# A recurrent attention block and an MLP in one kernel: twelve of sixteen sign steps of the weight conversion move from ScalarE to VectorE, more idle matmuls at the start, and a new written order for all engines

## The chip, the cores and the metric

One core of a Trainium2 chip. The time is device microseconds of one execution. The kernel before has a median of 570.65 us over 6 runs (570.09 to 571.48). The profile is of one execution of 571.31 us.

## The reference

```python
# gated linear attention, B=4, H=8, S=768, D=48, float32
state = zeros(B, H, D, D)
for t in range(S):
    state = alpha[:, :, t, :, None] * state + einsum('bhd,bhe->bhde', k[:, :, t], v[:, :, t])
    y[:, :, t] = einsum('bhd,bhde->bhe', q[:, :, t], state)
x = y.transpose(0, 2, 1, 3).reshape(3072, 384)
# MLP
h = x @ w_in                      # w_in 384 x 2048, float64 as handed in
g = h * clip(h + 3, 0, 6) / 6
out = g @ w_out                   # w_out 2048 x 384, float64 as handed in
```

The two weight matrices come as 64-bit floats. [...]the kernel loads each number as two 32-bit words and makes the float32 itself.

## The kernel before

**Chunks and groups.** The sequence is cut into 24 chunks j of 128 tokens (6 per batch); two chunks are a group g of 256 tokens, 12 groups. A chunk goes through the attention, a group through the MLP. All is float32.

**Attention of a chunk.** The scan of the decays is done within a chunk by VectorE: `r` (line 301, a scan backward, and a reciprocal in line 305) and `p` (line 312, a scan forward), then `k` and `q` scale the transposed keys and queries (line 324). TensorE makes the scores `sc` (line 332); VectorE masks them, `m` (line 338); TensorE makes the output within the chunk, `yi` (line 426), and from the carried state, `yx` (line 436); `kb` and `u` with VectorE's `sm` and GpSimd's `st` (line 383) carry the state. ScalarE copies the result to SBUF, `cy`. The first 6 chunks are transposed by TensorE (`ta`, `tk`, `tq`, line 274), later ones by VectorE (line 278).

**Weights.** They come in 16 slices of 128 x 768 numbers, 768 KB each: 0 to 7 are w_in (`w.0` to `w.7`, four DMAs each, line 174), 8 to 15 are w_out (one DMA each, line 177). A slice lands in one of five places, 0, 1, 2, 3, 4, 0, 1, 2 for slices 0 to 7 (3 and 4 lie in a tile, g_sb, that is free at the start), and 0, 1, 2 in turn after that; so slice 5 waits until slice 0 has been converted, 6 for 1, 7 for 2, 8 for 5, and so on. The conversion of slice i, with the names of the written order:

- `d2` (line 200, ScalarE): the size of the high word, read as a float, times 2^16, into the weight's place
- `d1` (line 189, ScalarE): the low word, scaled and rounded to an integer, in place
- `dx` (line 195, ScalarE): the sign of the high word, kept as a 16-bit half beside the low word
- `d3` (lines 208 and 209, VectorE): the size is clamped and shifted left by 3 bits
- `d4` (line 214, GpSimd): an integer add of low word and high part gives the float32

**MLP of groups 0 and 1.** These run while the weights arrive, as plain products. Step `f.g.i` (line 457) multiplies group g with slice i of w_in: 12 matmul records of 256 columns; `fa` and `fb` (line 468) do it for one chunk of group 0 at a time. ScalarE's `fr` and VectorE's `fg` apply the gate. Steps `b` (line 495) are w_out for group 0.

**MLP of the later groups.** It uses fewer products of sums. As the last `f` and `b` steps go by, VectorE turns w_in and w_out into sums in place: `y` (25 steps, lines 516 to 520) and `x.0` to `x.3` (line 626). From group 2 on the first matrix is the steps `M` (line 579, 128 columns), with sums of the inputs `xc` and of the results `o`; from group 1 on the second is the steps `P` (line 679, 192 columns), with sums `s`, copies `K`, outputs `G` and stores `O`.

**What sets the order.** One string of words near the end of the file (`run`), one word per step, gives the order in which the instructions of every engine and every DMA queue are issued; each engine works through its own in that order, and waits at the first whose inputs are not ready. All loads are issued by SP, one after the other; the stores by ScalarE's queue. The word `z.m.n` is `idle`: n matmuls whose result nobody reads, into PSUM bank m.

Of the kernel before, what the change touches and what calls it, by code (L numbers as in the profile page):

```python
# [17 lines left out]
def kernel(  # L18
# [32 lines left out]
    nc = tc.nc  # L51
# [81 lines left out]
    LOWEST, HIGHEST = 2.0, 2.0**16 * (122880.0 - 2.0**-7)  # L133
# [46 lines left out]

    def slice_of(i):
        dst, raw = weight_dst(i), raw_of(i)
        lo, hi = (raw[:, :, x].rearrange("p (m n) -> p m n", m=dst.shape[1]) for x in range(2))
        return dst, lo, hi
# [6 lines left out]
    def sign(i):  # L191

        dst, _, hi = slice_of(i)
        halves = raw_of(i).bitcast(F16).rearrange("p (m n) h -> p m n h", m=dst.shape[1])
        nc.scalar.activation(out=halves[:, :, :, 1], in_=hi.bitcast(I32), func=AF.Copy,
                             scale=2.0**-64)

    def magnitude(i):
        dst, _, hi = slice_of(i)
        nc.scalar.activation(out=dst, in_=hi.bitcast(FP), func=AF.Abs, scale=2.0**16)  # L200

    def magnitude_bits(i):

        dst, _, _ = slice_of(i)
        bits = dst.bitcast(U32)
        nc.vector.tensor_scalar(dst, dst, LOWEST, HIGHEST, ALU.max, ALU.min)
        nc.vector.tensor_single_scalar(bits, bits, 3, op=ALU.logical_shift_left)

    def add_low(i):

        dst, lo, _ = slice_of(i)
        nc.gpsimd.tensor_tensor(out=dst.bitcast(I32), in0=dst.bitcast(I32), in1=lo.bitcast(I32),  # L214
                                op=ALU.add)
# [291 lines left out]
    def idle(m, n):  # L507

        for _ in range(n):
            nc.tensor.matmul(bank_m[m][:, 0:C], ones[:, 0:C], ones[:, 0:C], start=True,  # L510
                             stop=True)
# [185 lines left out]
    def store2(g, i):  # L697
# [9 lines left out]
        "d1": round_low, "d2": magnitude, "dx": sign, "d3": magnitude_bits, "d4": add_low,  # L707
# [11 lines left out]
    def run(words):  # L719
        for word in words.split():  # L720
            name, *at = word.split(".")
            steps[name](*(int(x) for x in at))

    with tc.manual_schedule():
        run("""la.0 lk.0 lq.0 lk.1 ta.0 la.1 tk.0 la.2 ca.0 r.0 tq.0 lv.3.0 tk.1 lq.1 k.0 p.0 ta.1
            la.3 ca.1 ta.2 lv.0.1 q.0 ca.2 r.1 sc.0 lq.3 tq.1 lk.2 k.1 p.1 ta.3 la.4 z.0.2 r.2
            lv.1.2 ca.3 kb.0 w.1 z.0.1 q.1 ck.0 m.0 tk.2 u.0 k.2 sc.1 sm.0 p.2 tq.3 kb.1 lq.2
            z.0.2 m.1 st.1 ck.1 lk.3 ta.4 r.3 u.1 w.0 ca.4 yi.0 d2.1 sm.1 d1.1 d3.1 tq.2 z.0.1
            cy.0 dx.1 tk.3 q.2 st.2 lv.2.1 sc.2 k.3 d4.1 lq.5 kb.2 m.2 fa.1.0 w.2 r.4 d2.0 yi.1
            d1.0 d3.0 yx.1 dx.0 z.1.2 p.3 cy.1 w.3 fb.1 d4.0 q.3 sc.3 fr.0.1 p.4 d2.2 fa.0.1  # L730
            fg.0.1 d1.2 w.4 d3.2 tq.5 ck.2 fb.0 dx.2 m.3 d4.2 u.2 fr.0.0 yi.3 sm.2 d2.3 fg.0.0
            fa.2.2 st.3 lk.5 d1.3 d3.3 w.5 dx.3 yx.3 fb.2 cy.3 d4.3 d2.4 yi.2 d1.4 d3.4 tk.5
            fr.0.2 yx.2 lv.4.2 dx.4 fg.0.2 f.0.3.3 w.6 cy.2 d4.4 d2.5 f.1.2.0 d1.5 d3.5 fr.0.3
            la.5 dx.5 fg.0.3 w.7 f.1.3.1 d4.5 fr.1.2 fg.1.2 d2.6 d1.6 f.0.5.2 d3.6 fr.1.3 w.8
            dx.6 fg.1.3 d4.6 fa.4.3 fr.0.5 fg.0.5 kb.3 d2.7 fb.4 d1.7 d3.7 w.9 dx.7 f.0.6.0
            fr.0.4 d4.7 fg.0.4 d2.8 f.1.7.1 d1.8 d3.8 lk.4 fr.0.6 w.10 dx.8 fg.0.6 ck.3 f.1.6.2
            d4.8 fr.1.7 d2.9 fg.1.7 d1.9 d3.9 f.1.1.3 w.11 dx.9 fr.1.6 d4.9 fg.1.6 tk.4 d2.10
            ta.5 k.4 f.1.0.0 d1.10 w.12 d3.10 ca.5 dx.10 r.5 fr.1.1 u.3 fr.1.0 fg.1.1 d4.10
            f.0.7.1 d2.11 sm.3 lv.5.1 d1.11 k.5 st.4 fg.1.0 lq.4 dx.11 d3.11 f.1.5.2 fr.0.7 w.13
            fg.0.7 d4.11 d2.12 d1.12 b.0.0.3 d3.12 fr.1.5 dx.12 fg.1.5 w.14 d4.12 tq.4 f.1.4.0  # L740
            q.4 p.5 d2.13 d1.13 q.5 w.15 sc.4 d3.13 fr.1.4 dx.13 sc.5 m.4 d4.13 b.0.1 d2.14 m.5
            d1.14 la.6 d3.14 dx.14 kb.4 b.0.2 fg.1.4 d4.14 ck.4 lq.6 d2.15 d1.15 d3.15 u.4
            lv.6.0 dx.15 yi.5 sm.4 d4.15 lk.6 b.1.0.1 ca.6 r.6 lq.7 b.0.3 x.0 p.6 la.7 b.1.1
            tk.6 st.5 bo.0 so.0 y.1 k.6 y.5 yi.4 kt.6 b.1.2 y.6 kw.6 y.2 y.3 y.7 yx.4 y.4 y.8
            b.1.3 cy.4 tq.6 y.9 y.10 yx.5 y.11 bo.1 kr.6 x.1 P.1.1.2 so.1 cy.5 lk.7 s.1.0.0 x.2
            P.1.0.0 lv.7.1 s.1.1.1 la.8 x.3 M.2.15.3 K.1.0 s.1.2.2 u.6 P.1.3.1 s.1.3.3 s.1.4
            y.13 y.15 P.1.2 K.1.2 y.16 y.0 y.17 xc.2.1 y.12 M.2.16 K.1.1 xc.2.3 y.19 P.1.4
            xc.2.4 G.1.0 xc.2.5 O.1.0 y.20 s.1.5 M.2.0.2 q.6 G.1.1 sc.6 y.18 O.1.1 xc.2.6 y.21
            P.1.6 tq.7 y.23 xc.2.0 ca.7 P.1.5 G.1.3 xc.2.7 O.1.3 r.7 xc.2.8 p.7 M.2.7.0 n.2.0.8
            xc.2.9 M.2.1 sm.6 n.2.7.9 tk.7 st.7 M.2.8 n.2.1.10 o.2.4.0 M.2.2 k.7 e.2.4 M.2.17  # L750
            xc.2.2 xc.2.10 n.2.2.11 kt.7 M.2.3 y.14 kw.7 q.7 M.2.4 y.22 sc.7 G.1.2 n.2.4.12 y.24
            O.1.2 o.2.0.0 M.2.18.1 m.6 e.2.0 lq.8 M.2.9 n.2.18.13 h.2.0 M.2.5 o.2.1.0 M.2.19
            h.2.4 n.2.5.14 e.2.1 m.7 kr.7 M.2.10 M.2.6.2 lv.8.2 h.2.1 n.2.10.15 ca.8 yi.6 lk.8
            o.2.6.0 M.2.11 cy.6 r.8 yi.7 n.2.11.12 lq.9 o.2.5.0 M.2.12 p.8 e.2.5 yx.7 n.2.12.9
            h.2.5 u.7 la.9 cy.7 M.2.13 o.2.3.0 o.2.7.0 P.2.0.1 n.2.13.11 o.2.3.1 o.2.2.0 e.2.3
            o.2.7.1 h.2.3 e.2.7 M.2.14 o.2.2.1 K.2.0 h.2.7 e.2.2 M.3.15.3 o.2.6.1 h.2.2 e.2.6
            M.3.16 s.2.1.15 P.2.1.2 h.2.6 s.2.3.9 s.2.0.13 tq.8 P.2.3.0 s.2.2.11 s.2.4 tk.8
            P.2.2 K.2.2 xc.3.1 k.8 xc.3.3 kt.8 xc.3.4 kw.8 G.2.0 xc.3.5 O.2.0 s.2.5 M.3.0.2
            K.2.1 P.2.4 q.8 n.3.0.14 xc.3.6 tq.9 xc.3.0 ca.9 M.3.1 G.2.1 r.9 O.2.1 P.2.6
            n.3.1.12 kr.8 xc.3.7 p.9 lk.9 xc.3.8 M.3.2 sm.7 G.2.3 O.2.3 xc.3.9 sc.8 xc.3.2  # L760
            xc.3.10 n.3.2.10 q.9 lv.9.0 st.8 M.3.7.1 m.8 la.10 u.8 n.3.7.8 M.3.3 sm.8 M.3.8
            o.3.4.0 st.9 tk.9 e.3.4 M.3.4 h.3.4 P.2.5 n.3.4.13 k.9 o.3.0.0 kt.9 e.3.0 h.3.0
            M.3.9 kw.9 G.2.2 ca.10 sc.9 O.2.2 o.3.1.0 M.3.18.0 r.10 e.3.1 M.3.10 n.3.18.15 lq.10
            h.3.1 M.3.5 n.3.10.9 m.9 M.3.19 n.3.5.11 p.10 M.3.11 kr.9 M.3.6.2 o.3.6.0 n.3.11.8
            o.3.5.0 lv.10.1 M.3.17 o.3.7.0 e.3.5 lk.10 M.3.12 o.3.7.1 h.3.5 yi.8 e.3.7 n.3.12.13
            h.3.7 yi.9 lq.11 o.3.3.0 M.3.13 s.3.1.10 o.3.3.1 yx.9 n.3.13.15 s.3.3.9 la.11 yx.8
            e.3.3 o.3.2.0 cy.9 M.3.14 h.3.3 cy.8 o.3.2.1 u.9 o.3.6.1 P.3.0.0 e.3.2 tq.10 e.3.6
            h.3.2 h.3.6 P.3.1.3 tk.10 K.3.0 s.3.0.8 k.10 s.3.2.13 M.4.15.2 s.3.4 P.3.2 kt.10
            xc.4.1 kw.10 G.3.0 xc.4.3 O.3.0 s.3.5 P.3.3.1 K.3.1 xc.4.4 q.10 xc.4.5 tq.11 xc.4.6
            M.4.0.3 xc.4.0 K.3.2 ca.11 P.3.4 n.4.0.15 xc.4.7 r.11 kr.10 xc.4.8 p.11 lk.11 M.4.1  # L770
            G.3.1 sc.10 xc.4.9 O.3.1 sm.9 n.4.1.11 xc.4.2 P.3.6 xc.4.10 lv.11.2 q.11 m.10 st.10
            la.12 M.4.2 G.3.3 tk.11 O.3.3 lq.12 u.10 n.4.2.12 M.4.7.0 k.11 sm.10 M.4.3 n.4.7.14
            st.11 lv.12.0 M.4.16 ca.12 lk.12 M.4.4 o.4.4.0 M.4.8 r.12 n.4.4.9 e.4.4 sc.11 lq.13
            o.4.0.0 P.3.5 h.4.4 e.4.0 m.11 la.13 h.4.0 p.12 M.4.9 M.4.5 G.3.2 o.4.1.0 O.3.2
            M.4.18.1 tk.12 e.4.1 n.4.5.13 M.4.10 h.4.1 n.4.18.8 k.12 M.4.6.3 n.4.10.10 o.4.6.0
            M.4.19 kt.12 M.4.11 ca.13 kw.12 M.4.17 o.4.5.0 n.4.11.14 r.13 yi.10 e.4.5 M.4.12
            h.4.5 o.4.7.0 yi.11 n.4.12.9 o.4.7.1 M.4.13 o.4.3.0 e.4.7 yx.11 o.4.3.1 n.4.13.12
            h.4.7 yx.10 kr.12 e.4.3 o.4.2.0 cy.11 M.4.14 lk.13 h.4.3 cy.10 P.4.0.1 o.4.2.1
            s.4.1.10 e.4.2 o.4.6.1 lv.13.1 h.4.2 e.4.6 s.4.3.8 M.5.15.2 la.14 K.4.0 h.4.6
            P.4.1.3 tq.12 s.4.0.9 xc.5.1 s.4.2.14 s.4.4 u.12 P.4.2 xc.5.3 G.4.0 xc.5.4 O.4.0  # L780
            s.4.5 xc.5.5 P.4.3.0 q.12 K.4.1 xc.5.6 p.13 tq.13 M.5.0.3 K.4.2 xc.5.0 xc.5.8 xc.5.7
            P.4.4 xc.5.9 sm.12 n.5.0.12 tk.13 st.13 ca.14 M.5.1 k.13 G.4.1 sc.12 xc.5.2 O.4.1
# [107 lines left out]
```

## Time and profile before

| what | us |
|---|---|
| median of the runs | 570.65 |
| the profiled execution | 571.31 |
| its span, from the first to the last instruction | 569.5 |
| TensorE busy with matmuls | 550.2 |
| VectorE busy | 469.4 |
| ScalarE busy | 216.7 |
| GpSimd busy | 55.4 |

The granted TensorE clock has a mean of 0.997 over the span. Times in the tables are from the span's start. In a row of the costliest groups stand the line, the engine, the operation, what it writes and reads, the count, then the busy time in us and the mean of one in ns, then the idle time of that engine just before these instructions and what ended most of it. In the order of time, a row is start, duration, engine, line, and in brackets the idle time before it and what ended that. A busy TensorE row is not TensorE at its peak, since matmuls overlap. Each matmul of float32 leaves two records.

### The profile page before, as it was taken

What the parts mean: (1) busy time and instruction counts of PE and PEld (TensorE: products, weight loads), DVE (VectorE), ACT (ScalarE), POOL (GpSimd) and SP (SyncE); (2) the same over time, 40 slices, a digit from 0 to 9 for tenths busy, and PEclk for the clock granted to TensorE, in tenths of its full rate; (3) what the DMA queues carried; (4) which work ended last, traced back from release to release, by engine and by line L of the source; (5) the groups of instructions that cost most, each with busy time, mean ns of one, the idle gap of its engine ahead of it and who ended that gap; (6) DMA issues with size and microseconds to landing.
All of it is one profiled execution on the core that took longest, in us unless ns stands there. A gap on an engine that the chain in (4) does not pass through costs nothing.

```text
span 569.5 us, 12659 instructions
## 1 busy us (share of the span) xinstructions
PE 550.2 (97%) x5196; PEld 506.0 (89%) x5196; DVE 469.4 (82%) x786; ACT 216.7 (38%) x360; POOL 55.4 (10%) x70
## 2 busy tenths in 40 slices
PE   5699899999999999999999999999999999999997
PEld 3587786589999999989989989899899999999997
DVE  7785478999999999899699799989799787564580
ACT  2469999111442432341341341432431431442420
POOL 2225344300000000000001001000000000000000
PEclk9989999999999999999999999999999999999999
DMA  9999777440524535551650655041642630000000
GB/s 146 190 202 179 199 197 184 96 103 21 111 51 97 119 72 115 129 102 33 151 102 16 141 111 141 12 114 23 139 102 61 128 93 8 2 22 8 1 28 22
DMA packets 121270, 53.73 MB, mean 94 GB/s; under 512 B 80636, under 2 KB 114172, under 8 KB 121212
## 3 DMA queue, kind: packets, MB, share of 16 engines
q1 hardware_dynamic: 114588, 48.19, 41.7%
q10 hardware_dynamic: 6624, 4.72, 2.6%
q8 instruction: 41, 0.67, 0.5%
q14 instruction: 17, 0.14, 0.1%
HBM read 44.24 MB, written 8.65 MB: 93 GB/s over the span
## 4 chain that ended last, share of the span: by engine, by line
PE 72%; DVE 10%; DMA 9%; SPq 3%; issue 2%; ACT 2%; DVEq 0%; ACTq 0%
PE m_ps L679 30%; PE m_ps L579 28%; DMA raw<-in_moe_w_in_dram 4%; PE sc_ps L332 3%; PE y_ps L426 3%; PE m_ps L457 3%; PE y_ps L436 2%; DMA rings<-in_k_dram 1%; DMA g_sb<-in_moe_w_in_dram 1%; PE u_ps L396 1%; SPq L174 1%; SPq L253 1%; PE m_ps L495 1%; DMA kq<-in_k_dram 1%; DMA rings<-in_alpha_dram 1%
## 5 line engine op out<-in xcount | busy, mean ns | idle before, releaser
L679 PE MATMUL m_ps<-w,g_sb 128*128 128x192 f32 x704 | 121.7, 328 | 0.4 <-DVE g_sb L516 0.4
L679 PEld LDWEIGHTS m_ps<-w,g_sb 128*128 128x128 f32 x704 | 113.8, 190 | 2.2 <-issue 1.0
L585 ACT COPY g_sb<-m_ps 128x512 f32<-128x512 f32 x110 | 63.7, 583 | 108.5 <-PE m_ps L579 101.8
L679 PE MATMUL m_ps<-rings,g_sb 128*128 128x192 f32 x528 | 92.0, 327 | 0.0
L679 PEld LDWEIGHTS m_ps<-rings,g_sb 128*128 128x128 f32 x528 | 85.4, 190 | 0.7
L473 ACT ACTIVATE r<-g_sb,half 128x512 f32<-128x512 f32 x80 | 57.3, 722 | 75.0 <-DVE g_sb L520 28.0
L579 PE MATMUL m_ps<-xc,w 128*128 128x128 f32 x640 | 84.3, 278 | 0.5 <-DVE oh L695 0.5
L579 PEld LDWEIGHTS m_ps<-xc,w 128*128 128x128 f32 x640 | 78.1, 192 | 3.5 <-issue 1.4
L477 DVE SCALAR_TENSOR_TENSOR g_sb<-r,g_sb 128x512 f32<-128x512 f32 x80 | 54.5, 684 | 17.2 <-ACT r L473 13.0
L383 POOL TENSOR_TENSOR t<-t,R 128x384 f32<-128x384 f32 x20 | 19.6, 978 | 384.6 <-DVE t L411 261.9
L579 PE MATMUL m_ps<-xT,raw 128*128 128x128 f32 x400 | 51.7, 276 | 0.1
L579 PEld LDWEIGHTS m_ps<-xT,raw 128*128 128x128 f32 x400 | 48.7, 192 | 0.5 <-ACT g_sb L585 0.3
L579 PE MATMUL m_ps<-xT,w 128*128 128x128 f32 x320 | 42.1, 279 | 0.1
L626 DVE TENSOR_TENSOR g_sb<-g_sb 128x512 f32<-128x512 f32 (+1 forms) x55 | 41.5, 788 | 0.1
L579 PEld LDWEIGHTS m_ps<-xT,w 128*128 128x128 f32 x320 | 38.2, 192 | 2.0 <-ACT g_sb L585 1.3
L457 PE MATMUL m_ps<-xT,w 128*128 128x256 f32 x144 | 32.4, 381 | 1.6 <-POOL w L214 1.6
L338 DVE TENSOR_TENSOR A<-sc_ps,mask 128x512 f32<-128x512 f32 x48 | 30.7, 682 | 3.9 <-PE sc_ps L332 3.7
L579 PE MATMUL m_ps<-xc,raw 128*128 128x128 f32 x240 | 32.4, 278 | 0.2 <-DVE xc L518 0.2
L312 DVE TENSOR_TENSOR_SCAN P<-t 128x516 f32<-128x516 f32 x24 | 32.4, 1350 | 0.3
L516 DVE TENSOR_TENSOR g_sb<-g_sb 128x512 f32<-128x512 f32 x40 | 27.2, 682 | 6.5 <-ACT g_sb L585 6.5
L301 DVE TENSOR_TENSOR_SCAN R<-t,ones 128x516 f32<-128x516 f32 x24 | 30.4, 1265 | 2.0 <-ACT t L292 1.9
L457 PEld LDWEIGHTS m_ps<-xT,w 128*128 128x128 f32 x144 | 26.9, 190 | 5.7 <-POOL w L214 2.0
(104 smaller groups left out, 704.8 us busy)
## 6 DMA issues: line engine op xcount, KB each, us to landing
raw<-in_moe_w_out_dram SPq DMA_DIRECT2D x8, 768.0 KB, 4.3
t<-in_v_dram SPq DMA_DIRECT2D x48, 96.0 KB, 5.7
raw<-in_moe_w_in_dram SPq DMA_DIRECT2D x24, 192.0 KB, 8.0
out_dram<-oh ACTq DMA_DIRECT2D x44, 96.0 KB, 2.1
far<-kq SPq DMA_DIRECT2D x60, 64.0 KB, 2.3
kb<-far SPq DMA_DIRECT2D x15, 256.0 KB
aq<-in_alpha_dram SPq DMA_DIRECT2D x36, 96.0 KB, 4.0
qq<-in_q_dram SPq DMA_DIRECT2D x36, 96.0 KB, 2.8
```

Of the source, the lines that this page charges most:

```text
L301: nc.vector.tensor_tensor_scan(out=reverse(R, n - 1, n), data0=reverse(ax, n, n), data1=reverse(ones, n, n), initial=0.0, op0=ALU.mult, op ...
L312: nc.vector.tensor_tensor_scan(out=P_t[j], data0=aX[j % 2][:, 0:n], data1=ini[j % 2], initial=0.0, op0=ALU.mult, op1=ALU.add)
L338: nc.vector.tensor_tensor(out=A_t[j][:, NP * o : NP * (o + 1)], in0=ps_t.pop(("sc%d" % o, j)), in1=mask.unsqueeze(1).to_broadcast([C, NP, ...
L383: nc.gpsimd.tensor_tensor(out=st[j % 2], in0=sm[j % 2], in1=R_t[j][:, :, 0:1].to_broadcast([C, NP, 2 * D]), op=ALU.mult)
L457: nc.tensor.matmul(h[:, f], w1[:, kk, o : o + C], xT_t[g][:, kk], start=(kk == 0), stop=(kk == KT - 1))
L473: nc.scalar.activation(out=to, in_=h, func=AF.Relu, bias=half, scale=1.0 / 6.0)
L477: nc.vector.scalar_tensor_tensor(out=to, in0=r, scalar=1.0, in1=h, op0=ALU.min, op1=ALU.mult)
L516: eng.tensor_tensor(out=out, in0=in0, in1=in1, op=ALU.add if s1 > 0 else ALU.subtract)
L579: nc.tensor.matmul(acc[g][i][:, f * C : (f + 1) * C], spots[w][:, f * C : (f + 1) * C], x_of(g, x), start=(first and f == 0), stop=last, s ...
L585: nc.scalar.copy(out=slots[z], in_=acc[g][i])
L626: nc.vector.tensor_tensor(out=out, in0=in0, in1=in1, op=ALU.subtract)
L679: nc.tensor.matmul(to[g], a, rhs[:, f], start=(first and f == 0), stop=(last and f == HF - 1), skip_group_check=True)
```

## The change

Three edits.

1. For slices 0, 1, 2 and 4 the conversion stays as it was. For the other twelve `dx` is left out: `d2` takes the size without the factor, `d3` clamps it, shifts it and masks two bits in the same instruction, and a third VectorE instruction (scalar_tensor_tensor, 128 x 768 words of 32 bits) puts sign and top bit of the high word over it, written to the high word's place, every second word. `d4` then reads the high part from there.
2. The matmuls of `idle` multiply the identity matrix instead of a part of `ones` that is zero; there are 8 such steps with 28 matmuls instead of 5 with 8, the first of them right after the first load is issued.
3. The string with the order of the steps is another one. Its steps are the same, but for the twelve `dx` and the idle ones.

```diff
+    BY_HALVES = {0, 1, 2, 4}
+
...
     def magnitude(i):
         dst, _, hi = slice_of(i)
-        nc.scalar.activation(out=dst, in_=hi.bitcast(FP), func=AF.Abs, scale=2.0**16)
-
-    def magnitude_bits(i):
...
-        dst, _, _ = slice_of(i)
+        nc.scalar.activation(out=dst, in_=hi.bitcast(FP), func=AF.Abs,
+                             scale=2.0**16 if i in BY_HALVES else 1.0)
+
+    def high_bits(i):
+        dst, _, hi = slice_of(i)
         bits = dst.bitcast(U32)
-        nc.vector.tensor_scalar(dst, dst, LOWEST, HIGHEST, ALU.max, ALU.min)
-        nc.vector.tensor_single_scalar(bits, bits, 3, op=ALU.logical_shift_left)
+        if i in BY_HALVES:
+            nc.vector.tensor_scalar(dst, dst, 2.0**16 * LOWEST, 2.0**16 * HIGHEST, ALU.max,
+                                    ALU.min)
+            nc.vector.tensor_single_scalar(bits, bits, 3, op=ALU.logical_shift_left)
+        else:
+            nc.vector.tensor_scalar(dst, dst, LOWEST, HIGHEST, ALU.max, ALU.min)
+            nc.vector.tensor_scalar(bits, bits, 3, 0x3FFFFFF8, ALU.logical_shift_left,
+                                    ALU.bitwise_and)
+            nc.vector.scalar_tensor_tensor(hi, hi, 0xC0000000, bits, ALU.bitwise_and,
+                                           ALU.bitwise_or)
 
     def add_low(i):
 
-        dst, lo, _ = slice_of(i)
-        nc.gpsimd.tensor_tensor(out=dst.bitcast(I32), in0=dst.bitcast(I32), in1=lo.bitcast(I32),
-                                op=ALU.add)
+        dst, lo, hi = slice_of(i)
+        high = dst if i in BY_HALVES else hi
+        nc.gpsimd.tensor_tensor(out=dst.bitcast(I32), in0=high.bitcast(I32),
+                                in1=lo.bitcast(I32), op=ALU.add)
...
         for _ in range(n):
-            nc.tensor.matmul(bank_m[m][:, 0:C], ones[:, 0:C], ones[:, 0:C], start=True,
-                             stop=True)
+            nc.tensor.matmul(bank_m[m][:, 0:C], ident, ident, start=True, stop=True)
```

The constants LOWEST and HIGHEST lose their factor of 2^16. Of the order, the loads up to the last slice of w_in, with the small loads of chunks (`la`, `lk`, `lq`, `lv`: alpha, keys, queries, values; 192 KB each) between them:

```
before: la.0 lk.0 lq.0 lk.1 la.1 la.2 lv.3 lq.1 la.3 lv.0 lq.3 lk.2 la.4 lv.1 w.1 lq.2 lk.3
        w.0 lv.2 lq.5 w.2 w.3 w.4 lk.5 w.5 lv.4 w.6 la.5 w.7 w.8 w.9 lk.4 w.10 ...
after:  la.0 lq.0 lk.0 lk.1 la.1 lv.0 lq.2 la.2 lq.1 la.3 lv.3 w.1 lv.1 la.4 lk.2 w.3 lk.3
        lv.2 w.0 lq.3 w.4 lq.4 la.5 lk.5 w.2 w.5 lq.5 w.6 w.7 w.8 w.9 lk.4 w.10 ...
```

(The numeral after `lv` is the chunk; its ring slot is left out.) The products with w_in, groups 0 and 1:

```
before: fa.1 fb.1 fa.0 fb.0 fa.2 fb.2 f.0.3 f.1.2 f.1.3 f.0.5 fa.4 fb.4 f.0.6 f.1.7 f.1.6 f.1.1
        f.1.0 f.0.7 f.1.5 b.0.0 f.1.4 ...
after:  fa.1 fb.1 f.0.3 fa.0 fb.0 f.1.4 f.1.3 fa.4 f.1.2 fa.2 fb.4 f.0.5 f.1.5 fb.2 f.0.6 f.1.7
        f.0.7 f.1.0 b.0.0 b.1.0 f.1.1 f.1.6 ...
```

In both orders the 'ta', 'tk', 'tq', `sc`, `kb`, `u`, `yi` and `yx` of chunks 0 to 3, and transposes of chunks 4 and 5, stand between these.

## The prediction

> **What bounds the kernel now.** I read the page first, then stretches of 14 to 20 us, then the order of time around the first 105 us.
>
> ```profile
> PE   5699899999999999999999999999999999999997
> DVE  7785478999999999899699799989799787564580
> ACT  2469999111442432341341341432431431442420
> ```
>
> Each digit is a fortieth, 14.2 us. TensorE fills from the third digit on; holes to close are in the first 60 us alone. ScalarE is full in digits 4 to 7 (43 to 100 us), and nearly idle after them.
>
> ```profile
> 57.00:71.00 14.00, 12.40 (x72) 10.96 (x71) 7.07 (x10) 13.00 (x15) 4.59 (x4) 1.00 0.71 197
> 71.00:85.00 14.00, 14.00 (x83) 12.15 (x82) 9.84 (x17) 13.94 (x17) 6.70 (x5) 1.00 0.76 204
> 85.00:100.00 15.00, 14.61 (x112) 10.13 (x115) 13.12 (x18) 13.98 (x14) 7.55 (x8) 1.00 0.72 178
> ...
> 114.00:128.00 14.00, 14.00 (x115) 12.47 (x114) 14.00 (x18) 1.65 (x5) 0.00 (x0) 1.00 0.43 104
> ...
> 160.00:180.00 20.00, 19.78 (x134) 19.49 (x133) 19.49 (x35) 5.39 (x10) 0.00 (x0) 1.00 0.19 41
> ```
>
> Columns are PE, PEld, DVE, ACT, POOL busy us, clock, DMA share, GB/s. To 100 us ScalarE sets the pace of the weight conversion while VectorE idles (57 to 100 us: 30.03 busy of 43). From 100 us on VectorE and TensorE are both full: two engines are tied.
>
> ```profile
> 61.96 0.92 ACT L200 ACTIVATE w<-raw 128x768 f32<-128x768 f32 x1 [0.93 <-DMA raw<-in_moe_w_in_dram]
> ...
> 67.62 8.04 PE L457 MATMUL m_ps<-xT,w 128*128 128x256 f32 x36 [1.60 <-POOL w L214]
> ```
>
> The last w_in slice (7) arrives at 61.96 us; ScalarE waits for it, and TensorE waits for its last conversion step until 67.62.
>
> A busy PE row is no measure of its work, so I count matmul records at the distance of their starts in full stretches: 112 ns with 128 columns, 163 with 192, 216 with 256, 323 with 384 (small products by their groups: scores 1.16 us a chunk, within 1.05, across 0.8). So counted, 44.8 us of useful work lies in the order ahead of f.1.7, the first product of slice 7. It starts at 67.62: TensorE has lost 22.8 us by then. From there to 200 us it loses only some 4.7 more, about 3.5 of it the small seams that the later stretches show too.
>
> **The change, part by part.** The profiled execution took 571.31 us, 0.66 over the median of 570.65; its span is 569.5. A gain in its span is taken off the median.
>
> *Signs off ScalarE.* The page's rows for it:
>
> ```profile
> L195 ACT ACTIVATE raw<-raw 128x768 f16<-128x768 int32 x14 | 27.0, 1929 | 0.2
> L214 POOL TENSOR_TENSOR w<-w,raw 128x768 int32<-128x768 int32 x14 | 25.9, 1852 | 40.6 <-ACT raw L195 21.3 <-DMA raw<-in_moe_w_in_dram 11.9 <-DMA g_sb<-in_moe_w_in_dram 4.7
> ```
>
> 12 of 16 go: 12 x 1.93 = 23.2 us off ScalarE, from the stage that it fills. ScalarE is then no bound: a slice costs it 0.82 + 0.82 us, plus a gate.
>
> *Signs on VectorE.* 12 scalar_tensor_tensor of 768 elements. Two-input operations start 0.60 us apart with 512 elements, 1.13 with 1024, 1.67 with 1536 (L516, L626), so 0.87 us: 12 x 0.87 = 10.4 us. The nearest rows for stride are ScalarE's: L189 reads and writes every second word in 915 ns, as L200, which writes a dense tile, in 917; only the 2-byte write of L195 doubles. I take 0.87; the ends are 0.87 and twice that, since no VectorE row has this stride. The mask joined to the shift, the scale 1.0 and the other input of the integer add cost nothing: L208 runs two operations per instruction already, and the add already reads one strided input (ends: 0 to 0.3 us each on GpSimd, which has gaps of 1 to 3.5 us between adds).
>
> *What the new order does on TensorE.* In the SP order 10,176 KB stand ahead of the end of slice 7 both before and after, and from 15 to 57 us the queue moves some 190 GB/s, so slice 7 arrives at about 62 us again. Its conversion: 0.92 (L200), 0.6 + 0.6 + 0.87 on VectorE beside 0.9 on ScalarE, 1.85 on GpSimd: ready at 67.0 instead of 67.6. But the new order puts 50.8 us of useful work ahead of f.1.7, not 44.8: two more products of other slices, 5.2 us, and two transposes. Can TensorE have done them? w.1 stands after 2112 KB of small loads instead of 2688, three loads fewer at some 1.15 us each, so slice 1 is ready at about 26 us instead of 29.5; slices 3, 0 and 4 arrive 1 to 2 us earlier than the second to fourth slice before. The two tightest steps that I find: scores of chunk 3 behind the clamps of slices 3 and 0 on VectorE (start about 39 us with 22.0 us of work ahead) and fa.0 (slice 0 ready at 40.6, 23.6 ahead). Both leave a loss of 17.1; f.1.7 then starts at 67.9 to 68.3. By TensorE alone the gain is 22.8 - 17.5 = **5.3 us**.
>
> *What it does on VectorE.* Its work from the clamp of slice 7 (62.92 before) to x.0, the first w_out combination (103.91), summed at start distances: before 27.2 us in 41.0, the rest waits and slow instructions. After, the order holds 32.4 there: nine slices at 0.87 more is 7.8, less 2.6 for steps moved (scans, scales and masks ahead of slice 7 or behind x.0). It no longer waits for ScalarE; slots and landings can still cost about 1 us (three slots, a slice turning in 4.3 + 0.9 + 2.1 + 1.85 = 9.2, so 3.1 each, against some 3.6 of VectorE per slice).
>
> Here a rule speaks against the change.
>
> ```profile
> 100.84 1.84 POOL L214 TENSOR_TENSOR w<-w,raw 128x768 int32<-128x768 int32 x1 [1.12 <-ACT raw L195]
> ...
> 101.57 2.20 DVE L301 TENSOR_TENSOR_SCAN R<-t,ones 128x516 f32<-128x516 f32 x1
> ```
>
> The scan takes 1.23 elsewhere; here it ends when the add does. The Trainium skill ("SBUF — State Buffer", section "SBUF: two separate sides") says that VectorE instructions with two SBUF inputs or in a two-port mode and GpSimd instructions share one port pair, which the first holds for its whole length while the other is blocked. The new sign step is of that kind. By the rule at its worst, nine adds of 1.85 hold VectorE for 16.7 us. The rows say less: in the ten adds from 60 to 101 us the overlapping VectorE instructions ran 0.03 to 1.27 over their shortest, 4.4 us together, because gates that read PSUM often stand behind an add. VectorE will be fuller, and a clamp or scan follows the add more often: I take 6 us (ends 4 and 16.7). So x.0 comes at 62.9 + 32.4 + 6 + 1 = 102.3, and the rest of VectorE's work up to 200 us is the same sum within 1 us, less 0.7 of slow-downs beside the state product of chunk 5. By VectorE alone the gain is 1.6 + 0.7 = **2.3 us**.
>
> *Idle products.* 28 instead of 8, at 0.224 us: 4.5 us more of TensorE, all within the first 22 us of its useful work, where it stands still for some 16 us; if that cover were gone they would cost up to 4.5. What they can bring: the clock's half-rate window at 28 to 31.5 us (mean clock 0.88 from 28 to 42) stretched scores, a transpose and products by some 1.7 us, and the first twelve transposes ran at 272 ns instead of 157. Both lie ahead of the arrival of slice 7; I count 0 for the end (ends 0 and 1.5).
>
> *Waits on slots.* w.7 loads into the slot of slice 2, which now comes fifth instead of third: SP holds w.7 until slice 2's add ends, about 52.5 us. Before, its four issues ran from 50.4 to 53.1, with 9 us of queue ahead of the landing. I count 0; each us that slice 2 is later than about 54 us delays slice 7 and everything behind it on SP (w_out slices, chunk 6). From 200 us on the steps are the same in number; VectorE gains 2 to 10 us of lead on TensorE by 280 us, so nothing new is late there.
>
> **The sum.** The engines are tied: VectorE is idle 1.5 us of the 58 from 142 to 200, so the end follows neither alone. I take the middle of 2.3 and 5.3, 3.8 us: 570.65 - 3.8 = 566.9.
>
> **Rivals.**
> - TensorE alone decides (0.15): the gates find enough VectorE lead. 5.3 to 7 us with the clock's 1.5: 563.6 to 565.4. For it: VectorE idles 13 us between 57 and 100 today. Against: 14.00 of 14.00 right after.
> - The gain is eaten (0.16): slice 2's slot, or add hold-ups of 8 to 9 us instead of 6: gain within 0 to 1.6, 569.0 to 571.
> - Slower (0.06): the port pair. Adds and VectorE exclude each other nearly whole in slices 7 to 15. VectorE then carries 16.7 instead of 6: 10.7 more, minus 2.3 and minus the 1.5 spare gives some 7 us, 577.6. It decides from about 8.3 us of hold-ups by VectorE's sum, 0.92 per add against 0.44 in the rows. A strided sign step at 1.74 us would add as much.
> - The main case, 564.9 to 569.0, has 0.63.
>
> A measurement of this kernel can tell about 0.2%, 1.1 us, from no change. Faster by more than that, 569.5 or less: nearly all of the main case and the first rival, and some of the second: 0.85. Same 0.09, slower 0.06. Range: from TensorE alone to most of the eaten gain, 563.6 to 570.0.
>
> **What would show it.** ScalarE's row of signs has 4 instructions, its busy time falls by some 23 us, and digits 4 to 7 of its line are no longer full. VectorE from 63 to 103 us is near full. The new sign row has a mean near 0.9 to 1.0 us; over 1.5, the rival of the port pair or the stride is at work. The last wait of L200 on a w_in load ends at 61 to 63 us; 65 would be slice 2's slot. f.1.7 starts near 68 with no wait, the first w_out combination near 102. I am wrong if slice 7 arrives much earlier (the queue wasn't the bound), or if TensorE loses more after 200 us than before.

## The result and the profile after

The changed kernel has a median of 567.16 us over 17 runs (563.57 to 571.92), against 571.07 over 38 runs of the kernel before (569.27 to 572.80). The ratio is 0.9936, with a 95% interval of 0.9921 to 0.9952, so 3.9 us less. Run again beside three other kernels it had 568.35 against 570.45: 0.9961 (0.9944 to 0.9978). The gain holds in both; the ends of the two intervals put it between 1.3 and 4.5 us. In experiments 1, 6 and 12 one run, more than 1.5% above the fastest of its kernel, is left out of the ratio; without it their medians are 569.13, 567.20 and 568.09.

The profiled execution took 565.11 us, its span is 563.3, so it lies 2 us under its own median; the profiled pair differs by 6.2. Why these numbers differ is part of the explanation below.

First the slices of the page, 14.1 us each.

```profile
PE   7899999999899998999999999999999999999997
DVE  7776997999899999998998978976999977754580
ACT  1476655003322333323423422432421432432420
```

ScalarE's digits 4 to 7, full before, are now 6, 6, 5, 5. TensorE is full from the third digit; its digits 11 and 16 hold the small holes that come up again below. The same five stretches as before, in the same columns (PE, PEld, DVE, ACT, POOL busy us, clock, DMA share, GB/s):

```profile
57.00:71.00 14.00, 14.00 (x85) 12.85 (x85) 13.41 (x20) 10.43 (x15) 5.55 (x4) 1.00 0.75 205
71.00:85.00 14.00, 14.00 (x95) 10.65 (x94) 12.89 (x21) 7.64 (x10) 5.75 (x5) 1.00 0.66 192
85.00:100.00 15.00, 15.00 (x173) 10.52 (x172) 10.90 (x17) 7.99 (x13) 8.30 (x13) 1.00 0.78 202
114.00:128.00 14.00, 14.00 (x95) 14.00 (x94) 13.49 (x22) 0.95 (x3) 0.00 (x0) 1.00 0.04 14
160.00:180.00 20.00, 20.00 (x159) 19.48 (x159) 19.58 (x36) 3.36 (x8) 1.75 (x1) 1.00 0.27 62
```

TensorE has no idle time from 57 to 100 us (41.01 busy of 43 before); VectorE has 37.20 instead of 30.03 there, and still 5.8 to spare. The steps of slice 7, from the order of time of ScalarE and of TensorE:

```profile
60.87 1.00 ACT L207 ACTIVATE w<-raw 128x768 f32<-128x768 f32 x1
```

```profile
66.47 5.78 PE L471 MATMUL m_ps<-xT,w 128*128 128x256 f32 x26
...
111.04 1.14 PE L692 MATMUL m_ps<-w,g_sb 128*128 128x192 f32 x6
```

The first row is `d2` of slice 7: no bracket, so it did not wait for its load, which had landed a little earlier than forecast. The row at 66.47 is f.0.6 and then, from its 13th record at 216 ns each, f.1.7 at 69.06, with no wait before it. The last row is the first product P, which has 92.3 us of useful work ahead of it in both orders. In the kernel before it was

```profile
116.46 5.47 PE L679 MATMUL m_ps<-w,g_sb 128*128 128x192 f32 x32
```

so it now comes **5.4 us** earlier.

The groups of the conversion:

```profile
L202 ACT ACTIVATE raw<-raw 128x768 f16<-128x768 int32 x3 | 5.8, 1943 | 0.0
...
L221 DVE SCALAR_TENSOR_TENSOR raw<-raw,w 128x768 uint32<-128x768 uint32 x11 | 10.6, 961 | 0.8
L228 POOL TENSOR_TENSOR w<-raw 128x768 int32<-128x768 int32 x11 | 17.7, 1611 | 24.7 <-DVE raw L221 11.5 <-ACT r L487 4.9 <-ACT w L207 2.6
L228 POOL TENSOR_TENSOR w<-w,raw 128x768 int32<-128x768 int32 x3 | 5.5, 1847 | 12.8 <-ACT raw L202 12.8
```

(The twelfth new sign step and the fourth old one work in g_sb and have rows of their own.) The sign step takes 0.96 us. The last two rows are the same integer add: from two places of the raw tile it is faster, 1.47 us where nothing holds it up (1.61 in the mean), than from the weight tile and the raw tile, 1.85.

### The profile page after: what moved, and what is told of

The parts are those of the page before. It is cut to its first block, busy times and chain, and to the rows that moved or that the text cites. A ratio compares the mean times of both kernels' runs of the same rounds, so it can differ in the third digit from the quotient of the medians.

```text
span 563.3 us, 12762 instructions
## 1 busy us (share of the span) xinstructions
PE 550.7 (98%) x5236; PEld 509.8 (91%) x5236; DVE 469.9 (83%) x798; ACT 196.6 (35%) x348; POOL 54.7 (10%) x70
## 4 chain that ended last, share of the span: by engine, by line
PE 89%; DMA 7%; DVE 2%; SPq 1%; issue 1%; ACT 0%; DVEq 0%; ACTq 0%
PE m_ps L692 35%; PE m_ps L592 29%; PE m_ps L471 6%; PE y_ps L440 4%; PE m_ps L509 4%; PE sc_ps L346 4%; PE y_ps L450 2%; DMA rings<-in_alpha_dram 2%; PE m_ps L482 2%; PE u_ps L410 2%; DMA kb<-far 1%; DMA t<-in_v_dram 1%; DMA rings<-in_k_dram 1%; DMA far<-kq 1%; PE tk_ps L288 1%
## 5 line engine op out<-in xcount | busy, mean ns | idle before, releaser
L592 PE MATMUL m_ps<-xc,w 128*128 128x128 f32 x640 | 83.1, 278 | 0.2 <-ACT g_sb L598 0.2
L487 ACT ACTIVATE r<-g_sb,half 128x512 f32<-128x512 f32 x80 | 55.5, 719 | 56.2 <-DVE g_sb L529 22.7
L397 POOL TENSOR_TENSOR t<-t,R 128x384 f32<-128x384 f32 x20 | 20.9, 1043 | 383.7 <-DVE t L425 206.2
L529 DVE TENSOR_TENSOR g_sb<-m_ps,g_sb 128x512 f32<-128x512 f32 x30 | 20.4, 683 | 27.6 <-ACT g_sb L598 26.9
L592 PEld LDWEIGHTS m_ps<-xT,w 128*128 128x128 f32 x320 | 38.2, 192 | 1.2 <-issue 0.2
L592 PEld LDWEIGHTS m_ps<-xc,raw 128*128 128x128 f32 x240 | 29.9, 192 | 1.2 <-ACT g_sb L598 0.9
```

What stands on the lines that cost most here:

```text
L487: nc.scalar.activation(out=to, in_=h, func=AF.Relu, bias=half, scale=1.0 / 6.0)
L529: eng.tensor_tensor(out=out, in0=in0, in1=in1, op=ALU.add if s1 > 0 else ALU.subtract)
L592: nc.tensor.matmul(acc[g][i][:, f * C : (f + 1) * C], spots[w][:, f * C : (f + 1) * C], x_of(g, x), start=(first and f == 0), stop=last, s ...
```

## The experiments

Times are medians. Each ratio, with its 95% interval, is to the kernel before in runs on the same chip; it is not the quotient of the two medians, and lies up to 0.25% from it. Edits of the order are shown as words. None leaves out a part of the computation; the fifth repeats a step whose second pass changes no value.

**1. Idle products on zeros.** The changed kernel, its idle products on a tile of zeros that VectorE fills at the start.

```diff
-            nc.tensor.matmul(bank_m[m][:, 0:C], ident, ident, start=True, stop=True)
+            nc.tensor.matmul(bank_m[m][:, 0:C], zero, zero, start=True, stop=True)
```

> The kernel after with the idle matmuls on a tile of zeros (set by VectorE in its first instruction, 0.17 us) in place of the identity; same number, same places. If the clock follows how many matmuls run, whatever their numbers: as the kernel after, 566 to 568 us, mean clock 0.994 to 1.0. If it needs operands that are not zero: the clock is granted later or taken back more often in the first 30 us, 569 to 571 us, mean clock under 0.992.

Measured: 569.30, ratio 0.9959 (0.9941 to 0.9977). The first 140 us are those of the changed kernel (first P at 111.33). From first P to `P.4.0`, the first w_out product of group 4, its profile takes 4.1 us longer than that of the changed kernel: TensorE waits 2.88 us at 223 us, and half the clock follows. The changed kernel can lose as much there (experiment 12). Whether zeros or the identity are multiplied makes no difference that these runs can tell. Its time is in the range of the second expectation, its mean clock over the runs, 0.994, in that of the first.

**2. No idle products.** All eight words are taken out.

```diff
-z.3.5 ... z.0.2 ... z.0.1 ... z.0.5 ... z.0.2 ... z.0.4 ... z.0.4 ... z.0.5
```

> The kernel after with no idle matmul at all. By the prediction the idle products bring 0 to 1.5 us and cost nothing: 567 to 568.5 us. If the clock is what the runs of the kernel after differ by (spans 561.8 to 563.9 at mean clocks of 0.999 to 1.0, 569.6 and 570.1 at 0.988), then without them more half-rate windows fall into the first 45 us: 569 to 572 us at a clock of 0.985 to 0.990.

Measured: 570.13, ratio 0.9989 (0.9972 to 1.0006): no gain is left that can be measured. First P starts at 113.11 instead of 111.04. The stretches of the first 42 us, of this kernel and then of the changed one:

```profile
14.00:28.00 14.00, 9.76 (x148) 7.43 (x146) 13.60 (x18) 6.79 (x11) 3.57 (x2) 0.98 1.25 190
28.00:42.00 14.00, 13.70 (x152) 12.01 (x152) 9.53 (x17) 7.10 (x9) 4.47 (x4) 0.77 1.06 178
```

```profile
14.00:28.00 14.00, 12.06 (x170) 9.38 (x171) 10.84 (x16) 6.21 (x10) 3.58 (x2) 0.88 1.22 191
28.00:42.00 14.00, 14.00 (x186) 12.27 (x185) 10.95 (x19) 10.54 (x16) 4.94 (x4) 1.00 1.00 175
```

Both meet half the clock (0.77 from 28 to 42 us here, 0.88 from 14 to 28 in the changed kernel), but without the idle products for longer, and mostly behind 28 us, where TensorE has useful work.

**3. The new order with all signs on ScalarE.**

```diff
-    BY_HALVES = {0, 1, 2, 4}
+    BY_HALVES = set(range(16))
```

with a word `dx` put ahead of each `d4` that had none.

> The kernel after with all sixteen signs on ScalarE again (each right before its integer add), VectorE without its sign steps; order and idle matmuls stay. If ScalarE's relief carries the gain: ScalarE is full again from 43 to 100 us, the first w_out combination comes at 104 us or later, 570 to 572 us. If the order does it alone: 566.5 to 568 us.

Measured: 575.07, ratio 1.0096 (1.0059 to 1.0133), slower than before and above both expectations. TensorE, in order of time:

```profile
37.34 4.31 PE L471 MATMUL m_ps<-xT,w 128*128 128x256 f32 x12 [2.44 <-POOL w L228]
```

This is f.0.3, which the new order puts early: its slice isn't converted. The same wait stands ahead of f.1.7 (at 74.45, 0.98 us); x.0 comes at 110.24.

**4. The old order with the signs moved.** The conversion of the changed kernel in the order of before, less its twelve `dx`; idle products as before.

```diff
-... d3.3 w.5 dx.3 yx.3 ...
+... d3.3 w.5 yx.3 ...
```

> The order and the idle matmuls of the kernel before, with the twelve signs on VectorE (the words for the twelve sign steps taken out, nothing else moved). If the order is needed, since f.1.7 stands ahead of work that is ready: f.1.7 starts at about 67 us with 44.8 us of work ahead of it, 569.5 to 571 us. If ScalarE's relief is enough: 566.5 to 568.5 us.

Measured: 572.24, ratio 1.0022 (1.0012 to 1.0033), a little above the first expectation. f.1.7 starts at 66.70, 0.9 earlier than before, but x.0 at 104.66, 0.75 later: in the old order the relief of ScalarE hurries TensorE up to f.1.7, while VectorE, with twelve steps more, comes later.

**5. The sign step twice.**

```diff
-            nc.vector.scalar_tensor_tensor(hi, hi, 0xC0000000, bits, ALU.bitwise_and,
-                                           ALU.bitwise_or)
+            for _ in range(2):
+                nc.vector.scalar_tensor_tensor(hi, hi, 0xC0000000, bits, ALU.bitwise_and,
+                                               ALU.bitwise_or)
```

> The kernel after with each of the twelve sign steps on VectorE issued twice (the second writes the same values again): some 10.5 us more of VectorE, at slices 3 and 5 to 15. If VectorE is tied with TensorE up to 200 us, as the prediction has it, most of it comes out at the end: 571 to 577 us. If TensorE alone decides and VectorE has lead to spare: the first w_out combination about 8 us later than 101.2 us, and yet 567 to 569 us.

Measured: 575.21, ratio 1.0061 (1.0039 to 1.0083). At 0.88 us from start to start the twelve steps add 10.5 us to VectorE. First P starts 8.4 us later than in the changed kernel (119.41) and the median is 8.05 later (7.1 by the two ratios). Two stretches of this kernel:

```profile
71.00:85.00 14.00, 13.06 (x83) 10.21 (x81) 13.47 (x19) 7.72 (x12) 4.06 (x3) 1.00 0.67 196
85.00:100.00 15.00, 11.74 (x144) 8.50 (x145) 14.50 (x20) 6.83 (x10) 5.62 (x6) 0.94 0.54 165
```

VectorE is full (14.50 of 15) and TensorE stands still for 3.3 us. A half-rate stretch of 3.4 us begins there, too, and can account for 1.7 of the 8.4. So the changed kernel had 2 to 4 us of VectorE to spare ahead of first P, and TensorE set that point.

**6. Two state products later.** In the changed kernel TensorE waits 1.56 us at 143.37 and 1.50 at 221.73, both ahead of `u` (line 410), for keys that go to DRAM and back (`kr` reads them back). Here `u` of chunks 6 and 10 is put behind more work.

```diff
-... M.2.19 o.2.0.0 p.7 u.6 e.2.0 ... M.4.4 p.11 e.4.4 u.10 k.11 ...
+... M.2.5 tk.7 yi.6 u.6 o.2.1.0 ... la.13 M.4.17 u.10 o.4.1.0 ...
```

> The kernel after with the state products of chunks 6 and 10 (u.6, u.10) behind some 3 us more of TensorE's other work, so that the keys that they wait for are back from DRAM. If those two waits (1.56 and 1.50 us in the profile) cost only themselves: 1.5 to 3 us less, 564 to 566 us. If the wait at 221 us also costs the clock, as the half-rate windows at 222 to 232 us in two other profiles say: the same or more, 563 to 565 us, and in no run a mean clock under 0.993. If VectorE or something else is as late there: 567 us as before.

Measured: 568.19, ratio 0.9929 (0.9902 to 0.9956). Both waits are gone from the profile, but 1.88 us appear at 151.88 ahead of scores that wait for VectorE.

**7. The same, without the last idle step** (5 products in front of scores of chunk 3, whose queries were ready 0.25 us after they began).

```diff
-... yx.2 z.0.5 la.5 ...
+... yx.2 la.5 ...
```

> As the run with u.6 and u.10 later, and without the five idle matmuls ahead of the scores of chunk 3, which in the profile end at 40.06 us while the queries were ready at 39.0. If they held the scores up: another 0.5 to 1 us less. If they keep the clock, or the scores were not what is late next: the same within 0.5 us.

Measured: 566.58, ratio 0.9911 (0.9885 to 0.9936); the profile has first P at 111.21 and ends 0.4 us before that of the changed kernel. Six runs are too few to call it better.

**8. The kernel before, slice 7 later.** Slices 6 and 7 change places for group 1, so that TensorE no longer waits 1.60 us for slice 7.

```diff
-... f.1.7.1 ... f.1.6.2 ...
+... f.1.6.1 ... f.1.7.2 ...
```

> The kernel before with one edit of its order: slices 6 and 7 of w_in change places for group 1, so that f.1.7 comes one product (2.6 us) later. If the wait of 1.60 us at 67.62 us was a real loss of the old order: 569 to 569.7 us. If VectorE, full from 100 us on, is what the end follows: 570.3 to 571 us, no change.

Measured: 570.76 against 570.78, ratio 0.9999 (0.9987 to 1.0011). TensorE, in order of time:

```profile
63.03 9.23 PE L457 MATMUL m_ps<-xT,w 128*128 128x256 f32 x42
```

The wait is gone: products run from 63.03 to 72.26 without a break. First P starts at 113.99, 2.5 us earlier than before (part of that can be the clock, which is full throughout here and 0.88 from 28 to 42 us in the profile of before), and the last product ends at 565.02, 1.4 earlier than in the profile of before, but the median doesn't move. The wait that the profile of before shows most plainly was worth 0.7 us at most (the lower end of the interval), and by the median nothing.

**9. The kernel before with 28 idle products** on the identity.

```diff
-la.0 lk.0 ... z.0.2 ... z.0.1 ... z.0.2 ... tq.2 z.0.1 ... z.1.2
+la.0 z.3.5 lk.0 ... z.0.2 ... z.0.5 ... z.0.4 ... z.0.4 tq.2 z.0.5 ... z.1.3
```

> The kernel before with the 28 idle products of the changed kernel (on the identity, 5 of them after the first load, the rest in front of the steps where TensorE stood still: second, fourth and fifth of the old idle places, and the transposes of queries 2), its order otherwise kept. If idle products are worth some 3 us by themselves, as their removal from the changed kernel was: about 567.8, with the half-rate window at 28 to 31 us gone and a mean clock of .998 or more. If the old order is held by VectorE after 100 us, so that what TensorE gains early is lost again (as when slice 7 was put later): 570 to 571, first P product at 115.5 to 116.5 though the products of the first 60 us start up to 2 us earlier.

Measured: 571.26 against 570.45, ratio 1.0013 (1.0000 to 1.0027). One stretch of it:

```profile
28.00:42.00 14.00, 13.08 (x175) 11.23 (x178) 12.15 (x16) 9.45 (x12) 3.88 (x3) 1.00 0.97 189
```

The clock is 1.00 where before had 0.88. It brings nothing, as in the second expectation, but VectorE is not what stops it: f.1.7 starts at 67.35 (67.62 before), still after a wait of 1.13 us for its slice, so what TensorE gained ahead of it ends in that wait, and first P is at 116.18 (116.46).

**10. The sign step written to the weight tile.** The add then reads weight tile and raw tile, as before.

```diff
-            nc.vector.scalar_tensor_tensor(hi, hi, 0xC0000000, bits, ALU.bitwise_and,
+            nc.vector.scalar_tensor_tensor(bits, hi, 0xC0000000, bits, ALU.bitwise_and,
...
-        high = dst if i in BY_HALVES else hi
+        high = dst
```

> The changed kernel with one difference: the sign step writes its result over the dense weight tile instead of over every second word of the raw tile, and the integer add reads it from there. If the add's faster pace (1.47 us against 1.85) comes from reading both inputs out of the raw tile, it is back at 1.85 for all slices, twelve times 0.38 us of GpSimd more; GpSimd is no bound, so the end moves by the slices' delay alone, 0 to 1.5 us: 567.2 to 568.7. If the pace came from VectorE being elsewhere, the add stays at 1.47 and the time at 567.2. In both cases the sign row stays at 0.96 us.

Measured: 568.19 against 568.35 for the changed kernel on the same chip, ratio to before 0.9960 (0.9936 to 0.9984). The group of the add:

```profile
L228 POOL TENSOR_TENSOR w<-w,raw 128x768 int32<-128x768 int32 x14 | 27.6, 1972 | 36.6 <-DMA rings<-in_q_dram 10.0 <-DVE w L221 9.9 <-ACT raw L202 5.1
```

The layout does set the add's pace: it is back at 1.85 us where nothing holds it up (1.97 in the mean), the first of the two theories. VectorE's instructions beside adds and other GpSimd work up to 150 us ran some 7 us over the shortest of their form, together, against some 3 in the changed kernel and 8.5 before: eight clamps (L218) ran over 0.25 us long, against one in the changed kernel. x.0 came 1.2 us later. The end shows none of it.

**11 and 12. Experiment 7 again, and the changed kernel again,** on the chip of experiment 10.

> The kernel with u of chunks 6 and 10 put behind work that covers the read-back of their keys, and without the last idle step, once more and beside the changed kernel. If the two waits (1.56 and 1.50 us) and the half-rate windows behind them are what spreads the changed kernel's runs: 565.5 to 566.6, 0.6 to 1.6 under it, with fewer runs of a mean clock under .995. If they are taken back elsewhere: within 0.5 us of it.

> The changed kernel itself, for the comparison with the three others on the same chip: about 567.2, between 564 and 572, runs of mean clock .999 or more near 564.7 and of .994 or less near 568.8.

Measured: 568.96 (13 runs), ratio 0.9956 (0.9937 to 0.9976), and 568.35 (22 runs), ratio 0.9961 (0.9944 to 0.9978). So moving the two state products gains nothing that can be measured, which is nearer to the second of the two expectations. What experiment 7 seemed to have gained is gone. Two profiles of the same changed kernel now lie side by side. TensorE ahead of `u` of chunk 10, in the first one:

```profile
221.73 0.56 PE L410 MATMUL u_ps<-t,kb 128*48 128x48 f32 x16 [1.50 <-DMA aq<-in_alpha_dram]
222.22 1.16 PE L346 MATMUL sc_ps<-q,k 48*128 48x128 f32 x16
223.31 1.16 PE L592 MATMUL m_ps<-xT,w 128*128 128x128 f32 x8
```

and in the second:

```profile
223.38 0.56 PE L410 MATMUL u_ps<-t,kb 128*48 128x48 f32 x16 [3.06 <-DMA aq<-in_alpha_dram]
223.88 2.08 PE L346 MATMUL sc_ps<-q,k 48*128 48x128 f32 x16
225.89 2.07 PE L592 MATMUL m_ps<-xT,w 128*128 128x128 f32 x8
```

with the stretch around it:

```profile
220.00:240.00 20.00, 16.94 (x186) 15.75 (x186) 15.85 (x26) 6.08 (x10) 2.11 (x2) 0.83 0.37 88
```

The wait is 1.56 us longer, and then scores and products take twice their time: the granted clock is 0.83 in the stretch of 220 to 240 us. From 0.1 us apart at 210 us the two profiles go to 4.6 apart at `P.4.0` (246.40 and 250.96), and are 4.9 apart at the last product. The releaser named is the last transfer to land; `u` reads kb, whose own transfer is the one to look at. SP's queue, in the first and in the second profile:

```profile
210.41 3.22 SPq L267 DMA_DIRECT2D kq<-in_k_dram  x4
213.67 1.86 SPq L267 DMA_DIRECT2D qq<-in_q_dram  x4
215.63 0.57 SPq L391 DMA_DIRECT2D kb<-far  x1
```

```profile
209.85 5.20 SPq L267 DMA_DIRECT2D kq<-in_k_dram  x4
215.09 1.86 SPq L267 DMA_DIRECT2D qq<-in_q_dram  x4
217.06 0.57 SPq L391 DMA_DIRECT2D kb<-far  x1
```

In the new order the read-back of chunk 10's keys stands on SP behind eight loads of chunk 11, keys and queries; in the old order it followed at once on the write of these keys, with the loads of chunk 11's queries ahead of both and those of its keys behind. Inside the key loads SP waits, 1.4 us in the first profile and 3.4 in the second, by the trace for an output store to land. In both `u` starts 6.1 to 6.3 us after the read-back is issued; in the old order it stood 9.4 us behind (216.30 and 225.71) and did not wait. In experiment 11 `u` no longer waits, but the loads are as late, and VectorE has it:

```profile
227.82 1.11 DVE L292 STREAM_TRANSPOSE k<-kq 128x512 f32<-128x512 f32 x1 [2.02 <-DMA kq<-in_k_dram]
```

So it looks as if SP's queue were the cause, and not where `u` stands. This is not shown: an order with the read-back ahead of chunk 11's loads was not tried.

## Why the prediction was right, and where it was not

**The size came out by luck.** 3.8 us was forecast, 3.9 measured (2.1 beside experiment 12). The step said: the engines are tied, the end follows neither alone, so take the middle of 2.3 and 5.3; behind 200 us it counted nothing. The profiled pair shows three terms in its place. Up to first P the gain is 5.4, TensorE's own sum (24.2 us lost before it, 18.7 after). For the rest take `P.4.0`, which has the same products ahead of it in both orders, and the last product. They start so, in the kernel before:

```profile
249.46 2.77 PE L679 MATMUL m_ps<-w,g_sb 128*128 128x192 f32 x16
...
563.64 2.76 PE L679 MATMUL m_ps<-rings,g_sb 128*128 128x192 f32 x16
```

and in the changed kernel:

```profile
246.40 5.47 PE L692 MATMUL m_ps<-w,g_sb 128*128 128x192 f32 x32
...
557.49 2.76 PE L692 MATMUL m_ps<-rings,g_sb 128*128 128x192 f32 x16
```

At `P.4.0` the gain is 3.1: 2.4 of the 5.4 are given back, where the two new waits ahead of `u` (1.56 and 1.50 us) stand. At the end it is 6.2: another 3.1 are gained behind `P.4.0`, where the prediction had 0. This last term is the later order's. From the start of `P.4.0` to the end of the last product all ten profiles with the new order take 313.9 to 314.6 us, the four with the old order 316.2 to 317.2. TensorE counts as busy nearly throughout in both (309.52 and 310.00 of the 310 us from 250 to 560), so no open wait went away; where the 3.1 us come from was not followed. So the rival "TensorE alone decides" has the time of this execution, 565.11, in its range, but its sum did not have these terms either.

The median is higher since in many of its runs, by the profiles, the new order loses more at 222 us. The prediction had written "nothing new is late there", and named a greater loss after 200 us as a sign of being wrong; it came true in the profiles with a long wait there (experiments 1, 2 and 12), not in the profiled pair. In the profile of experiment 12 `P.4.0` starts 1.5 us later than before, and what is left of the gain at the last product, 1.3, comes from behind it. Of 18 executions of the changed kernel four had a mean clock of 0.999 or more, with a median of 564.7, and eight 0.994 or less, with 568.8. Of 51 runs of before beside experiments 1 to 4 (those beside the changed kernel have no clock on record), 23 were in the first class at 570.2 and 15 in the second at 571.6. So the gain is some 5.5 us where the clock is not reduced, and about 2.8 where it is. In experiment 12 the same classes give 3.4 and 1.6: both smaller there, for a reason that stays open, but in the same order. That runs of low clock are those with a long wait at 222 us is shown by profiles only: waits of 1.2 to 1.5 us there (the changed kernel, experiments 3 and 5) were followed by no reduced clock, 2.00 us (experiment 10) by one stretch of 3.4 us at half rate, 2.88 to 3.06 us (experiments 1, 2 and 12) by one of 6.8.

**Signs off ScalarE: right.** 20.1 us fewer (23.2 were taken out; 3.1 came back in longer rows of other steps, which was not followed), and ScalarE ceased to be a bound. Experiment 3 shows that the new order needs this, experiment 4 that the signs alone gain nothing. Neither was a step of the sum, since it took both together.

**Signs on VectorE: right.** 0.87 us from start to start was forecast, 0.88 measured; the stride of every second word costs nothing that shows. **The add** was taken as unchanged at 1.85, with ends of 0 to 0.3 above it. It went the other way, to 1.47 where nothing holds it up; experiment 10 shows that the layout did it. Being off the path it was worth nothing at the end.

**Hold-ups between VectorE and GpSimd: mis-sized.** 6 us of VectorE were taken; the trace has some 3 up to 150 us. By the Trainium skill ("SBUF — State Buffer", section "SBUF: two separate sides") whichever of the two starts first keeps the shared ports for its whole instruction. The new sign steps say nothing on this, since none of the twelve ran beside an add. But the rule shows the other way round, on GpSimd, for which the prediction had no term:

```profile
64.31 1.23 DVE L326 TENSOR_TENSOR_SCAN P<-t 128x516 f32<-128x516 f32 x1
```

```profile
64.53 2.27 POOL L228 TENSOR_TENSOR w<-raw 128x768 int32<-128x768 int32 x1 [2.40 <-DVE raw L221]
```

The add starts behind a scan and takes 0.80 us more than its 1.47, and so does the one at 55.65; the one at 43.99, of the old form, takes 0.79 more than its 1.85. That VectorE is held up less than before takes the new order and the faster add together: experiment 10 (new order, slower add) has some 7 us, experiment 4 (old order, faster add) some 6.6. x.0 came at 101.20, not 102.3.

**TensorE up to f.1.7: nearly right.** 17.5 us of loss was forecast, 18.3 measured: f.1.7 starts at 69.06 instead of 67.9 to 68.3. Behind it the changed kernel loses 0.4 us to first P where before lost 1.4, which the sum had not followed. That restores the 5.4.

**Slot of slice 2: right at 0.** SP issued w.7 at 53.27, and slice 7's first step, at 60.87, did not wait for its load.

**Idle products: mis-sized.** 0 was taken, with ends of 0 and 1.5. Without them the changed kernel is at 570.13 instead of 567.16: 3.0 us, or 1.6 by the ratio of experiment 12. On the chip of experiment 2 the kernel of experiment 1 is the nearest to compare with, and against it the difference is 0.8 by the medians and 1.7 by the ratios. So they carry some 1 to 3 us: 2.1 at first P by the two profiles, and what the clock loses besides (mean over the runs 0.990 without them, 0.995 in the changed kernel). The step failed because it took the arrival of slice 7 as the cover, as in the kernel before. There that holds: experiment 9 gave the old order the same idle products, the clock rose to 1.00 and nothing came of it. In the new order, with 50.8 us of work ahead of f.1.7, TensorE is behind and every lost us counts.

**Slower by the port pair** did not happen; its sign, a sign row over 1.5 us, is absent, and experiment 5 shows what it would have looked like: 10.5 us more on VectorE make 7 to 8 at the end.

## What to carry to other kernels

A wait that the profile shows openly can be worth nothing, here with a second engine full right behind it (experiment 8), and two changes that each bring nothing or harm (experiments 3, 4, 9) can gain together. When a new order is judged, follow the loads on the issuing queue as well as the engines: here one read-back moved behind eight loads, and TensorE then waited 1.5 to 3.1 us ahead of the product that reads it. Compare two profiles at several points that have the same work ahead of them, not at the end alone: here 5.4 us were gained, 2.4 given back and 3.1 gained again. One profiled execution can lie 2 us off its own median; look at the mean clock and the time of all runs before taking a difference of two profiles for the gain.

## What the runs showed of the hardware that was not expected

- An integer add of 768 elements on GpSimd takes 1.47 us with both inputs in the tile of interleaved words, and 1.85 with one of them in a dense tile, where nothing holds it up. Beside a scan of VectorE that started first it takes 0.8 us more.
- Behind 200 us, waits of TensorE of 2 to 3 us were followed by 3.4 or 6.8 us at half the clock, so they cost up to twice their own length (3.06 us of wait, and 3.4 us of stretched work behind it). The length alone does not settle it: 3.05 us at 97 us in experiment 5 were followed by 3.4 us, 1.88 us at 151.88 in experiment 6 by none, and 1.73 us at 27 us, in the kernel before, by 3.4. The Trainium skill ("TensorE: Matmul & The Clock Gate", section "Part 1: The HAM clock gate") has windows of about 3.4 us for this, which agrees (every such stretch in these profiles, but for those that the end cuts off, is 3.41 or 6.83 us long), but names a whole idle window as the trigger; here 2.00 us were enough.
- Idle products on zeros and on the identity could not be told apart, in the clock or in the time.
